# A delta-rule attention and an MLP-mixer on one core: multiplication and addition of an inversion step as separate pieces, and all pieces issued in another order

## The chip, the cores and the metric

The kernel runs on one NeuronCore of one Trainium2 chip. A core has engines that work side by side, each through an instruction queue of its own and in order: TensorE (PE; the loading of its weights is listed as PEld) multiplies matrices into PSUM, VectorE (DVE), ScalarE (ACT) and GpSimd (POOL) work on tiles in SBUF and PSUM, and SyncE (SP) issues the DMAs. The metric is device time in microseconds (us), from start to end of one execution. It is taken in runs of the whole kernel; one execution is also recorded by the hardware profiler, and all rows quoted below come from such a record. TensorE's clock is throttled at times; the granted clock is given as a share of full speed.

## The reference, cut to what matters

Two blocks follow each other, with batch 4, 8 heads, 768 positions, head size 48 (so model width 384), 256 hidden units over tokens and 1536 over channels, all in float32:

```python
k_n = k / (np.linalg.norm(k, axis=-1, keepdims=True) + 1e-06)
for t in range(S):
    kt, vt, bt = (k_n[:, :, t], v[:, :, t], beta[:, :, t, None])
    y[:, :, t] = np.einsum('bhd,bhde->bhe', q[:, :, t], state)
    v_old = np.einsum('bhde,bhd->bhe', state, kt)
    state = state + bt[:, :, :, None] * np.einsum('bhd,bhe->bhde', kt, vt - v_old)
...
xt = x.transpose(0, 2, 1)                  # x: y as (batch, position, 384)
h = np.maximum(xt @ w_tok1, 0.0) @ w_tok2
u = x + h.transpose(0, 2, 1)
h2 = np.maximum(u @ w_ch1, 0.0) @ w_ch2
return (u + h2).astype(np.float32)
```

## The kernel before, in words

**Blocks of the attention.** The positions are cut into chunks of 64, and two chunks make a unit of 128; 4 batches have 24 units, numbered 0 to 23. The effect of one chunk on the state is written with a 64x64 triangular matrix per head, made from the products of the keys with each other, which has to be inverted. So each unit passes these stages, each a generator in the code, and each named by a letter with the unit's number:

- k, `load_kq` (L409 ff., L444): SP loads the keys and queries; the keys also go into a staging tile `kst`.
- p, `prep`: the keys' norms and factors. Its last piece (L592) writes the scaled keys from `kst` into the unit's matrix; for units 0 to 3 it runs on DVE, for the others on POOL.
- c and d, `grams` (L511, L517): TensorE multiplies keys and queries with keys, DVE masks and scales.
- t, `to_parts`: the 32x32 diagonal blocks are put together for the inversion, for units 0 to 5 with copies, for the others with DMAs into a DRAM buffer (`n_dram`).
- i, `invert`: the inversion. It works on rounds of several units: i0 holds units 0 to 3, i1 units 4 and 5, i2 units 6 to 9, i3 10 to 13, i4 14 to 17, i5 18 to 21, i6 22 and 23. All of it is on DVE. Step s multiplies (L739) a column by a row into `sub` and adds (L744) that to the tile `x`. i0 and i1 have 14 such steps, the others 30; the tile has up to 128x240 elements in the middle steps.
- f, `from_parts`, h, `join_16`, j, `join`: the results come back (for later units by DMAs from `w_dram`), and the larger blocks of the inverse are made of them on TensorE, ACT and DVE.
- v, `load_v` (L460, L484): SP loads the values, POOL scales them.

**The recurrence.** r0 to r23 are the chunks of batches 0 and 1, one after the other (`recur`, L920 to L985); r24 to r35 those of batches 2 and 3, two at a time (`recur_pair`, L1009 to L1070). In each, TensorE multiplies the state with keys (`p_k`), DVE subtracts the values, TensorE multiplies by the inverse (`p_w`, first line L944), ACT copies that out of PSUM (L950), TensorE makes the change of the state (`p_s`), DVE subtracts it from the state (L967), and ACT writes the output rows.

**The mixer.** m0 and m1 (`mixer`) are batches 0 and 1; their pieces are put between those of the attention. Batches 2 and 3 are the end of the kernel: T2 and T3 for the part over tokens, A0 to A3, F0 to F3 and B0 to B3 for the part over channels (two units of positions each, with fewer and larger products made of sums; lines L1498 to L1700). w0 to w33 bring in the weights, one 128x384 or 128x256 piece each (`round_weights`): a DMA into one of three buffers `d`, two ACT passes (L286, L287), a DVE shift (L289) and a POOL addition (L293). q and s put aside and sum weights; b is beta; W, S and l belong to the end. x, z and Y are multiplications whose results nobody reads; they keep TensorE busy while nothing else is ready.

**What sets the order.** One string, `order`, lists the pieces by name, `i0*9` for nine pieces of i0, and a loop at the end of the kernel (L1867 ff.) takes one piece of the named generator for each:

```python
for word in order.split():
    name, _, n = word.partition("*")
    for _ in range(int(n or 1)):
        next(jobs[name])
```

A piece is what lies between two `yield`s. Its instructions go to the ends of their engines' queues, so the string is the order in every queue, the DMAs of SP included: an instruction waits for its inputs and buffers, and everything behind it on its engine waits with it. In `invert` one piece is the product and the sum of one step. The weight pieces, keys, queries, values, and the round trips of the inversions all share SP's queue.

Of the kernel before, what the change touches and what calls it, by code (L numbers as in the profile page):

```python
# [23 lines left out]
def kernel(  # L24
# [692 lines left out]
    def invert(rnd):  # L717
# [17 lines left out]
        for s in range(1, m - 1):  # L735
# [8 lines left out]
            nc.vector.tensor_tensor(  # L744
# [1138 lines left out]
```

## Time and profile before

| | |
|---|---|
| median of 3 runs | 624.91 us |
| lowest and highest run | 623.32 and 626.13 us |
| profiled execution: span, first to last instruction | 619.7 us |
| profiled execution: its own time around the span | not listed |
| TensorE busy | 590.3 us (95%), 8733 instructions |
| VectorE busy | 469.1 us (76%), 1160 instructions |
| ScalarE busy | 256.9 us (41%), 682 instructions |
| GpSimd busy | 109.9 us (18%), 150 instructions |
| mean granted TensorE clock | 0.975 |

The span is counted between the first and the last instruction on the core's engines; the time of a run includes what lies around it, so the median is 5.2 us above the span of this execution. An instruction's duration in the profile is that of one execution; a row that ends in x178 is a group of 178 instructions with their sum and mean. A busy engine isn't an engine that is needed: TensorE counts as busy at a low clock too, and with the multiplications that nobody reads.

### The profile page before, as it was taken

How to read it: one execution, taken by the hardware profiler on the slowest of the kernel's cores; microseconds unless marked ns; L12 is line 12 of the kernel's file. 1: busy time of each engine (PE TensorE's matmuls, PEld its weight loads, DVE VectorE, ACT ScalarE, POOL GpSimd, SP SyncE). 2: the span in 40 equal slices, each digit the busy share in tenths (PEclk: the TensorE clock that was granted, in tenths of full speed). 3: DMA queues.
4: the chain of work that ended last, by engine and by line, in shares of the span. 5: the costliest groups of instructions: out<-in, count | busy, mean ns of one | idle time of the engine just before them, and what ended most of it. 6: DMA issues, size and time to landing. Idle time of an engine off the chain costs nothing.

```text
span 619.7 us, 20909 instructions
## 1 busy us (share of the span) xinstructions
PE 590.3 (95%) x8733; PEld 515.9 (83%) x8733; DVE 469.1 (76%) x1160; ACT 256.9 (41%) x682; POOL 109.9 (18%) x150
## 2 busy tenths in 40 slices
PE   8588997999999999999999999999999999999998
PEld 5467875667898988877889888897699999999997
DVE  5987875986889855697566996866888898685874
ACT  8758796448521344223551215415352331414200
POOL 2348264225311122003020120010000000000000
PEclk9878797999999999999999999999999999999999
DMA  9667567667653254454445443135102012020001
GB/s 219 136 135 169 138 142 185 129 155 179 126 114 72 67 116 83 95 113 99 92 87 126 83 95 83 32 66 140 32 2 39 1 21 47 12 52 13 14 26 51
DMA packets 154605, 55.52 MB, mean 90 GB/s; under 512 B 129648, under 2 KB 148976, under 8 KB 154512
## 3 DMA queue, kind: packets, MB, share of 16 engines
q1 hardware_dynamic: 154512, 54.20, 39.1%
q8 instruction: 68, 1.11, 0.8%
q14 instruction: 25, 0.20, 0.1%
HBM read 41.19 MB, written 11.21 MB: 85 GB/s over the span
## 4 chain that ended last, share of the span: by engine, by line
PE 74%; DVE 9%; DMA 4%; ACT 4%; issue 2%; SPq 1%; POOL 1%; DVEq 0%; POOLq 0%; ACTq 0%
PE p_c L1668 13%; PE p_r L1498 13%; PE p_o L1689 10%; PE p_a L1570 7%; PE p_b L1570 6%; PE p_g L511 3%; DMA d<-in_moe_w_ch_dram 3%; PE p_h L1608 3%; DVE sub L739 2%; PE p L1593 2%; DVE x L744 2%; PE p_k L920 2%; PE p L1223 1%; PE p_h L1238 1%; PE p_y L1034 1%
## 5 line engine op out<-in xcount | busy, mean ns | idle before, releaser
L1668 PE MATMUL p_c<-u_t,wc 128*128 128x256 f32 x432 | 101.6, 386 | 0.5 <-issue 0.5
L1668 PEld LDWEIGHTS p_c<-u_t,wc 128*128 128x128 f32 x432 | 79.6, 190 | 11.9 <-issue 1.1
L1689 PE MATMUL p_o<-wc,r 128*128 128x192 f32 x360 | 64.6, 331 | 0.7 <-DVE xb L1628 0.7
L739 DVE TENSOR_TENSOR sub<-x 128x84 f32<-128x84 f32 (+24 forms) x178 | 58.4, 328 | 7.4 <-DMA x<-n_dram 2.8
L744 DVE TENSOR_TENSOR x<-x,sub 128x84 f32<-128x84 f32 (+24 forms) x178 | 58.2, 327 | 6.1
L1689 PEld LDWEIGHTS p_o<-wc,r 128*128 128x128 f32 x360 | 58.4, 190 | 2.3 <-DVE xb L1628 1.3
L1677 ACT ACTIVATE r<-p_c 128x512 f32<-128x512 f32 x36 | 21.4, 596 | 51.2 <-PE p_c L1668 46.1
L511 PE MATMUL p_g<-kq 48*64 48x128 f32 (+1 forms) x704 | 34.9, 283 | 4.0 <-ACT kq L587 3.3
L517 DVE TENSOR_TENSOR gm<-p_g,mb 128x512 f32<-128x512 f32 x44 | 28.9, 683 | 8.1 <-PE p_g L511 7.5
L484 POOL TENSOR_TENSOR v_st<-v_st,nrm 128x384 f32<-128x384 f32 x12 | 10.3, 856 | 131.9 <-DMA v_st<-in_v_dram 104.4
L574 POOL TENSOR_TENSOR mb<-mask_c,cs 128x512 f32<-128x512 f32 x20 | 21.2, 1062 | 67.8 <-DVE cs L552 36.9
L511 PEld LDWEIGHTS p_g<-kq 48*64 48x64 f32 (+1 forms) x704 | 26.5, 137 | 7.6 <-ACT kq L587 4.3
L293 POOL TENSOR_TENSOR wc<-w_f,d 128x384 uint32<-128x384 uint32 x24 | 24.6, 1029 | 42.8 <-ACT d L287 14.1
L1511 DVE TENSOR_TENSOR kq<-kq,p_r 128x384 f32<-128x384 f32 x40 | 21.0, 551 | 10.7 <-PE p_r L1498 8.8
L1498 PE MATMUL p_r<-t_d,wc 128*128 128x192 f32 x160 | 28.8, 326 | 0.0
L1511 DVE TENSOR_TENSOR gm<-gm,p_r 128x384 f32<-128x384 f32 x40 | 21.1, 551 | 8.1 <-PE p_r L1498 5.8
L400 DVE STREAM_TRANSPOSE kq<-pads 128x512 f32<-128x512 f32 x24 | 25.5, 1108 | 2.0 <-PE p_w L1038 1.6
L1498 PEld LDWEIGHTS p_r<-t_d,wc 128*128 128x128 f32 x160 | 26.5, 190 | 0.0
L1689 PE MATMUL p_o<-wc,s 128*128 128x192 f32 x144 | 25.7, 330 | 0.6 <-DVE xb L1628 0.6
L1498 PE MATMUL p_r<-pads,wc 128*128 128x192 f32 x128 | 25.4, 326 | 0.0
L1628 DVE TENSOR_TENSOR xb<-xb,p_o 128x192 f32<-128x192 f32 x42 | 14.6, 348 | 13.0 <-PE p_o L1689 12.6
L1689 PEld LDWEIGHTS p_o<-wc,s 128*128 128x128 f32 x144 | 23.3, 190 | 1.2 <-DVE xb L1628 0.9
(315 smaller groups left out, 1387.1 us busy)
## 6 DMA issues: line engine op xcount, KB each, us to landing
d<-in_moe_w_ch_dram SPq DMA_DIRECT2D x24, 384.0 KB, 4.2
v_st<-in_v_dram SPq DMA_DIRECT2D x96, 48.0 KB, 2.9
out_dram<-xb SPq DMA_DIRECT2D x23, 192.0 KB, 2.1
kst<-in_k_dram SPq DMA_DIRECT2D x64, 48.0 KB, 2.8
n_dram<-gm SPq DMA_DIRECT2D x72, 32.0 KB, 2.3
pads<-in_k_dram SPq DMA_DIRECT2D x24, 96.0 KB, 2.9
pads<-in_q_dram SPq DMA_DIRECT2D x24, 96.0 KB, 2.7
gm<-w_dram SPq DMA_DIRECT2D x72, 32.0 KB, 2.3
```

The lines of the kernel that those rows point to most:

```text
L293: nc.gpsimd.tensor_tensor(out=dst.bitcast(U32), in0=f, in1=lo, op=ALU.add)
L400: nc.vector.transpose(kq_of[p // 2][:, i, :, p % 2].rearrange("f p (s g) -> f p g s", g=G), rows_of[i].rearrange("s p (g d) -> s p g d", g ...
L511: nc.tensor.matmul(p_g[PAR[i ^ cc ^ swap(u)], p], kqt[f, p, cc, 0], kqt[f, p, cc])
L517: nc.vector.tensor_tensor(out=blocks(gm_of(u))[:, :, cc, D:GW].rearrange("s p (two n) -> s p two n", two=2), in0=p_g, in1=made[u][:, :, cc ...
L739: nc.vector.tensor_tensor(out=tmp, in0=y[:, :, 0:s, s : s + 1].to_broadcast([n, k, s, w]), in1=y[:, :, s : s + 1, s + 1 : m].to_broadcast( ...
L744: nc.vector.tensor_tensor(out=y[:, :, 0:s, s + 1 : m], in0=y[:, :, 0:s, s + 1 : m], in1=tmp, op=ALU.add,)
L1498: nc.tensor.matmul(p[:, i], pieces[q // width][:, at : at + 128], f[f"u{n}"], start=first and i == 0, stop=True, skip_group_check=True,)
L1511: nc.vector.tensor_tensor(out=o, in0=o, in1=p, op=op_of(sign))
L1570: nc.tensor.matmul(p, a[:, i], w[:, i // 2, i % 2], start=first and i == 0, stop=True, skip_group_check=True,)
L1668: nc.tensor.matmul(p_c[:, k], piece_of(wc1, cb, f * 128)[:, f * 128 : (f + 1) * 128], u_t[:, cb], start=(cb == 0), stop=(cb == NCB - 1),)
L1677: nc.scalar.activation(r2[:, m], p_c, ACTF.Relu)
L1689: nc.tensor.matmul(p, a[:, m], wc2[:, m, j], start=(start and i == 0), stop=(i == NM - 1), skip_group_check=True,)
```

## The change

In `invert` a `yield` stands between the multiplication and the addition of a step. So a round of inversion has one more piece for each step: i0 and i1 31 in place of 17, the others 62 in place of 32. The order string is another one throughout, with 2788 pieces in place of 2610; apart from those 178 pieces of the inversions each name occurs as often as before. The instructions, their shapes and their tiles stay as they are. Lines after L743 move down by one. The first part of the string, about as far as r11, is shown in both versions, and the end.

```diff
--- before.py
+++ after.py
@@ -741,6 +741,7 @@
                 in1=y[:, :, s : s + 1, s + 1 : m].to_broadcast([n, k, s, w]),
                 op=ALU.mult,
             )
+            yield
             nc.vector.tensor_tensor(
                 out=y[:, :, 0:s, s + 1 : m], in0=y[:, :, 0:s, s + 1 : m], in1=tmp,
                 op=ALU.add,
@@ -1773,76 +1774,95 @@
     jobs["z"] = keep_warm(4)
     jobs["y"] = jobs["Y"] = warm_tiles()
     order = """
-    w10 x*4 z w10*2 z w1*4 k1*3 z k1*3 z b p1 z p1 k0*6 p0*2 b*2 p1 w2 p0*5 p1*2
-    w10 p0*2 z w3 w2 c0*3 p0 w3*2 d0*2 w3 c0 p1 c0 d0*3 k2*3 v1 p1*2 w18 k2*2 p1*2
-    c1*2 d1 k2 p2*2 c1 t0 d1 c1*2 d1*3 t0 p2*8 c2*2 w2 d2 c2*3 Y d2 w2 k3*6 p3
-    d2*2 p3 d2 t1*3 x p3*7 c3 k4*5 k7 w13 w18*2 d3*2 v1*2 v0*2 c3*3 v0 c3 d3*3 t0
-    p4*2 t2*3 x t3*2 p4*2 x t3 i0*2 w13 p4*2 w18 w17*2 i0 k4 i0*9 p4 i0*2 p4*2 c4
-    k8 c4*3 w13*2 w6*2 k5*2 v0 k6 k5*2 i0*2 d4*2 k5 x z d4*3 c4 z*2 p5*2 k5 t4 p5
-    h0 h1 h0 w8*2 h1 Y i0 f0 Y p4 f1 h2*2 p5*3 f0*2 w6 h0*5 k6*5 p6 z f2*2 k8*3 p5
-    w6 p5 p3 p5 j0*3 f1*2 h1*5 j0*2 w8*2 w17 f2 h2*3 v0 t4*2 w17 r0*5 p6 h2*2 c5*2
-    v1 w11*2 j1 p5 k7*2 c5 k7 c5 r0 c5 r0*2 w14*2 v1 w11*2 k7*2 p7 d5*5 r1*5 w14*2
-    p6*2 t5 j1 t5*2 r1*2 j1 j2 p7 h3*2 r1*3 p6*3 i1*2 r2*5 k8*2 f3*2 w9 k9*3 j1*2
-    v2*2 i1*3 j2*2 r2*2 f3 i1*2 p6*3 w16 v2 w16*3 r2*2 h3 r2 i1 d6 r3*5 i1*2 w9*3
-    v2 d6 h3 v2 w0 h3*2 r3 h3 d6*2 w0 d6 j3 c6*5 r3*4 w0 j2 w0 p8*2 j2 r4 p8 r4*4
-    k9*3 j3*2 r4*2 i1*2 w24 i1*2 p7*7 r4 c7 r4 r5*5 k10 p9 k10 p9 c7 r4 c7*3 i1
-    w5*2 p7 r5*2 w24*3 r5*3 j3*2 i1 r6*4 w26 v3*5 p9 k11 r6 d7*5 w26*3 p8*3 t6*2
-    r6*2 w5*2 p8*4 v4*2 t6 i1 r6*3 h5*2 h4*2 k10*2 f4*3 c8*2 k10 p10 w28*2 c8*2 r7
-    c8 r7*3 d8*4 p9 d8 w28 h4*5 p9 t6 r7*2 j4 w28 p9*3 r7*2 p9 w7 d9 w7 v4*2 f5*2
-    w27*2 w7*2 d9*4 c9*2 f5 c9*3 t7*2 t8 r7*2 t7*2 j4*2 v4 p10*2 h5 r8*3 w29 t8*3
-    w29 w27*2 r8*2 w29*2 q3 w29 j4*2 r8 w22*4 t9*3 r8*3 p9 r9 p10 r9*3 t9 v5 h5*3
-    j5 i2 r9 w4*2 r8 h5 i2*5 w4 i2 w19*2 k10 w32 p10*2 w32 v7 k12 m0*2 k11 k12 q0
-    v5*3 p10*2 r9*2 j5*2 k11*3 i2*2 r9 w4 i2 j5 i2*3 p10 v5 r9*2 d10*3 r10 v7*2 j5
-    i2*2 r10*4 w12 i2 k12 i2*2 m0 w32 k11 k12 w32 r10*2 m0 p11 k12*4 w19 p11 r10
-    c10 r10 c10 r10 w33 d10*2 q2 Y r11*4 v7 r11*3 w19 c10 q1 w30 c10 r11 k12*2
-    i2*3 r11 v6*4 i2*5 m0*3 i2*5 q5 i2 m0 p11*4 c10 p11 m0 p11*2 m0*2 k12*2 w12
-    m0*3 v6 f6*3 w12 d11 c11*2 d11*2 c11 w33 c11 d11*2 j6 p12 w12 m0 w33 w30*3
...
-    A3*7 B2*5 A3 B2*2 A3*4 F2*2 F3 B2*7 F3*2 B2*2 F3*2 B2 F3*3 B2*6 F3 F2*2 B3*2
-    F3 B3*10 F3 B2*2 B3*5 F3*4 B3*13
+    x*7 k1 w1 k1 Y k0 k3 k0 k1*4 p1*2 w1*2 b z*2 k3 z*3 k0*4 p0*2 w1 p1 p0 w3 b*2
+    w3 p1 w3*2 p0*3 x p0*4 w2 z p1 d0*5 p1 c0 k2*6 k5 w2 c0*3 w10 c0 p1 k4 p1*2
+    c1 d1*4 p1 k3 p2*2 d1 t0*2 k3 k5 c1*3 p2 k3*2 p2 c1 t0 p2*3 w18 k4 p2 k6 p2
+    c2 d2*3 c2 p2 c2 w10 p3 w10 d2 w2 k4*2 d2 v0 t1 k4 p3*2 w2 k6*2 w10 v1 c2 w6
+    p3 c2 t1*2 p3*5 d3*2 c3 d3 c3*2 w18 c3 w18 d3*2 c3 t2 p4*2 v0 t2*2 t3*2 p4*2
+    k5 k7 k5 t3 i0 k5 w13 i0*4 w18 i0*3 p4 i0*7 w13 w17*2 p4 k4 p3 k7 p4 w13 w6
+    i0*2 p4*2 i0 k8 i0*2 p4 k8*2 i0 d4 v1 k6 k5 d4*2 i0 d4 z i0 z*2 k6 i0*2 c4 i0
+    c4*2 k8 i0 v1 i0 c4 i0*2 w6 w13 d4 c4 t4 h1 v1 h0 h1 w8 h0 p5 i0 p5 f1 f0 w6
+    f0*2 w17*2 Y w11 t4 f1 h2*2 p5*4 h0*2 k6 h0 p5 h0 z j0*2 h0 k7 w8 f2 w8 f1 h1
+    f2*2 j0 h1*3 j1 h1 v0*2 v1 v0 p6 w8 j0*2 p5*3 h2*3 r0*4 h2 r0 p6 c5*2 h2 c5*3
+    k8 r0*2 w14 d5*2 r1*2 p6 k8 w11 d5*2 p6 r1*2 w11*2 r1 d5 j1 k7 k9 k7 k9 p7*2
+    r0 r1 w14 t4 w14 t5*3 h3 r1*2 j2 j1 r1 p6 i1 h3 f3 r2*2 i1 f3*2 p6 j1 j2 j1
+    j2 p6*2 r2 r1 r2 w16 p6 i1 h3 i1 v2 w9 i1*2 p8 w16 h3 d6 r2 i1 r2 v2 i1 v2*2
+    i1*3 d6 r2 h3 i1 r2 d6*2 w16 h3 k10 p6 k10 i1 w14 r2 w0 h3 k9*3 i1*2 k7 c6 w9
+    c6 i1 r3 k10 w16 r3*2 r2 r3 w24 r3 Y w0*2 w9 k10 r3 w9 i1 d6 i1 v3 p7 v3 r3
+    v2 r3*2 j3 c6*3 r3 j2*2 r4 v3 r4*4 i1*6 w0 j3*2 r4*2 i1 w24 p7 i1 p7 r4*2 k10
+    r4 p7*3 p8 r5*4 t6 p9 r5*2 v3 p7 v3 i1 w24 i1 r5 c7*4 k9 r5 i1 c7 r5 r6 p8 r5
+    j3*2 r6 w26 i1 d7 r6 w24 w5 r6*2 v4 d7*3 w26*2 v4*2 d7 w26 p8*4 r6 w5*3 r6
+    p8*3 h5 p9*2 h5 h4 r6 i1 p10 d8*3 h4 t6 d8 f4 t6*2 f4*2 c8*3 r6 v4*2 d8 c8
+    w28 w7 p7 r7*2 w27 r6 r7 w28 r7*2 h4*3 c8 h4*2 t7*3 t8*4 w28*2 p9 r7 p10 r7
+    p9*4 r7 p9 w7 j4 w29 t7 r7 q3 c9*5 d9*5 t9 w7 w27*2 r8*2 f5 t9 r8 j4*2 t9*2
+    f5 j4 r7 f5 j4 p10 r8 w27 r8 w22 w7 p10 r8*2 w4 h5 w29*2 r8*2 r9 h5 r9*3 h5*2
+    j5 w29 j5 w22 j5 r8 w29 r9 w4 w22 i2 h5 w32 i2*3 k10 m0 v6 i2*5 p10 v5 j5 w4
+    i2*4 r9*2 i2*3 Y w22 w19 i2*2 v5 p10 i2*3 r9*2 v5 i2 v5 k12 p10 i2*2 w4 w32
+    k12 j5 k12*2 p10*2 r9 v5 m0 q2 r10 i2 k11*2 w19 r10*4 m0 i2 r10 i2*3 d10*2
+    c10*3 r10 i2*2 r10 c10 r10 k11 m0 k11*3 r11*2 v6 r10 r11 i2 r11 d10 i2*3 r11
+    i2*2 d10 w19 v6 i2*2 Y i2*2 w32 i2*3 k12 i2*3 d10 k12 w30 k12 v7 i2*2 v7 i2
+    r11 v6 r11 i2 q0 r11*2 m0 k12*2 i2*3 w19 i2*2 m0 w32 w33 m0 i2 w12 v7*2 p11
+    i2 q1 i2*2 w30 i2*2 m0 k12 p9 w12 k12 p11 f6 p11 m0 c10 p11*3 m0*2 p11 m0 p11
+    f6*2 p11 w12 w30 f7 w12 m0*2 d11 c11 d11*3 v7 f7*2 w15 c11 w30 f6 d11 j6 f8
...
+    A3*4 B2 A3*3 F2 A3*3 F2*2 A3*2 B2*2 A3*12 F2 A3*12 B2*9 F3*2 B2*4 B1 B2*3
+    F3*3 F2 B2*2 F3 B2*3 F3*2 B2 F3*3 B2 B3*3 F3 B2 B3*4 F3*3 B3*23
     """
     for word in order.split():
         name, _, n = word.partition("*")
```

In the old string the loads and preparations of units 0 to 3 come first, and the first steps of i0 (`i0*2 w13 ...`) in its fifth line; in the new one k1 and w1 come first, keys of units 4 to 7 come earlier, and i0 begins in the seventh line.

101 lines of the change are left out of this document (57 added, 44 removed).

## The prediction

> **What bounds the kernel now.** I read the page first (busy time, slices, chain), then busy time and granted clock by stretches, and then the order of time of single engines where a stretch had holes.
>
> ```profile
> PE 590.3 (95%) x8733; PEld 515.9 (83%) x8733; DVE 469.1 (76%) x1160; ACT 256.9 (41%) x682; POOL 109.9 (18%) x150
> PEclk9878797999999999999999999999999999999999
> PE 74%; DVE 9%; DMA 4%; ACT 4%; issue 2%; SPq 1%; POOL 1%; DVEq 0%; POOLq 0%; ACTq 0%
> L739 DVE TENSOR_TENSOR sub<-x 128x84 f32<-128x84 f32 (+24 forms) x178 | 58.4, 328 | 7.4 <-DMA x<-n_dram 2.8
> L744 DVE TENSOR_TENSOR x<-x,sub 128x84 f32<-128x84 f32 (+24 forms) x178 | 58.2, 327 | 6.1
> ```
>
> TensorE is busy for 95% of the span and carries 74% of the chain. The two lines of the inversion step (L739 multiplies, L744 adds) run 178 times each, a third of a microsecond apiece.
>
> The next rows give, for each stretch, busy time on PE, PEld, DVE, ACT and POOL, then the granted clock, the DMA share and GB/s.
>
> ```profile
> 0.00:20.00 20.00, 16.61 (x197) 11.82 (x197) 11.86 (x40) 16.80 (x45) 4.63 (x17) 1.00 0.81 185
> 20.00:40.00 20.00, 12.31 (x95) 7.76 (x94) 17.80 (x50) 9.93 (x23) 8.97 (x11) 0.74 0.72 164
> 40.00:60.00 20.00, 16.98 (x502) 15.19 (x504) 16.27 (x29) 16.91 (x49) 14.20 (x18) 0.96 0.66 142
> 60.00:80.00 20.00, 18.70 (x539) 16.35 (x535) 16.44 (x48) 16.04 (x46) 7.36 (x10) 0.78 0.58 137
> 80.00:100.00 20.00, 17.73 (x559) 15.38 (x552) 15.14 (x34) 17.58 (x46) 13.08 (x16) 0.99 0.68 154
> 100.00:120.00 20.00, 16.61 (x303) 11.71 (x304) 15.55 (x47) 9.81 (x27) 4.77 (x7) 0.76 0.67 163
> 120.00:440.00 320.00, 314.76 (x5504) 264.81 (x5497) 238.22 (x610) 120.16 (x347) 56.91 (x74) 1.00 0.46 101
> 440.00:620.00 180.00, 176.56 (x1068) 172.85 (x1067) 137.85 (x308) 49.64 (x105) 0.00 (x0) 1.00 0.11 24
> ```
>
> This splits the kernel in two. From 120 us on, TensorE is short of full by 320 - 314.76 = 5.2 us up to 440 and by 3.4 us after it, with the clock at 1.00. No order of the same matmuls can win more there than these 8.7 us. Before 120 it is idle for 120 - 98.9 = 21 us, and the clock is down to 0.74, 0.78 and 0.76 in three of the six stretches. So the end is set by **how early the full stretch begins**, and this hangs on the recurrence steps r0 to r11, with DVE, ACT, POOL and the one DMA queue of SP around them.
>
> **The change, part by part.**
>
> *The yield.* It adds no instruction: the orders hold the same pieces, except that i0 and i1 grow from 17 to 31 and i2 to i6 from 32 to 62, 178 more, one for each L739. Its own cost is 0: DVE, which executes them, gets the same 1160 instructions. What it can give is that an urgent DVE piece stands behind one half of a step and not a pair, 0.4 us for the longest steps (rows below).
>
> *The order up to r0.* The first 120 us have nearly the same pieces in both orders, moved by a few places, but the SP queue differs. I counted its DMAs: the transfer that w13 waits for goes from 22nd to 33rd, that of w17 from 28th to 34th, the queries of block 4 from 29th to 35th, the last values of block 0 (needed by r0) from 34th to 52nd. In front now stand the keys of blocks 5 and 6 and w6. On DVE, p3's last piece (L592) and w13's shift now stand inside the first inversion, after its 14th half step; p3's stood behind the inversion.
>
> ```profile
> 12.36 0.55 DVE L592 TENSOR_TENSOR wc<-kst,cs 128x384 f32<-128x384 f32 x1
> 46.13 1.15 POOL L293 TENSOR_TENSOR w<-w_f,d 128x384 uint32<-128x384 uint32 x1 [0.35 <-issue]
> 46.42 1.29 DVE L592 TENSOR_TENSOR gm<-lent,cs 128x384 f32<-128x384 f32 x1
> 29.80 0.60 SPq L444 DMA_DIRECT2D kst<-in_k_dram  x1
> d<-in_moe_w_ch_dram SPq DMA_DIRECT2D x24, 384.0 KB, 4.2
> 32.58 0.28 DVE L739 TENSOR_TENSOR sub<-x 128x112 f32<-128x112 f32 x1
> 47.76 1.91 SPq L444 DMA_DIRECT2D lent<-in_k_dram  x3
> v_st<-in_v_dram SPq DMA_DIRECT2D x96, 48.0 KB, 2.9
> 51.11 0.83 POOL L460 TENSOR_TENSOR v_st<-v_st,nrm 128x384 f32<-128x384 f32 x1
> 52.00 0.68 PE L944 MATMUL p_w<-v_st,wc 64*64 64x48 f32 x15
> 52.00:99.00 47.00, 42.74 (x1272) 37.71 (x1270) 36.92 (x92) 40.18 (x109) 26.85 (x34) 0.89 0.68 157
> ```
>
> The first inversion: L592 costs 0.55 us (alone) to 1.29 us (beside POOL). The Trainium skill, "SBUF — State Buffer", section "Who interferes with whom", says that a VectorE instruction with two SBUF inputs and a GpSimd instruction that reads SBUF exclude each other; the 1.29 beside POOL's L293 agrees, and by it this item would be 0.7 us dearer wherever POOL is running. The 33rd DMA was issued at 29.80; with 4.2 us to landing, w13's data is there at 34.0, ACT's first pass adds half a microsecond, and DVE stands at this place at 32.6 + 0.55. So DVE waits up to 1.4 us and the first inversion ends 0.55 to 2.0 us later than before. Queued behind it are t16 and with it h0, j0 and r0.
>
> The values of block 0: the 52nd DMA was issued at 48.4 (second of the row at 47.76). With 2.9 us to landing and 1.0 us for POOL's two instructions (the longer one is the 0.83 at 51.11), r0 starts at 52.3 where it started at 52.00; POOL now also takes block 1's values first, about one more: 53.3. Both paths meet in r0, so the larger counts, not the sum: +0.3 to +2.0, I take +1.2. Between 52 and 99 the busiest engine after TensorE, ACT, has 47 - 40.18 = 6.8 us without work; a late r0 can be made up there. I keep **+0.5** at r8, between 0 (all hidden) and +2.0 (cover gone). Bounds of the start itself (k1's keys are now the first DMA, two weight transfers later): ACT is busy 16.80 of the first 20 us, and the same ACT pieces stand before the first inversion in both orders, so 0.
>
> *The order from r8 to r11*, where I see the gain. The window rows have the columns of before; the others are start, duration, engine.
>
> ```profile
> 99.00:102.00 3.00, 0.99 (x30) 0.63 (x26) 0.72 (x2) 1.07 (x3) 0.59 (x1) 0.59 0.30 55
> 102.00:105.00 3.00, 2.12 (x48) 1.88 (x48) 0.99 (x4) 1.01 (x5) 2.47 (x3) 0.50 0.70 193
> 105.00:108.00 3.00, 3.00 (x10) 2.08 (x9) 2.56 (x11) 1.05 (x4) 0.37 (x1) 0.50 1.00 299
> 108.00:111.00 3.00, 3.00 (x14) 1.61 (x12) 2.79 (x9) 2.08 (x5) 0.97 (x2) 0.71 1.00 232
> 101.02 0.55 ACT L286 ACTIVATE d<-d 128x384 f32<-128x384 f32 x1 [1.93 <-DMA d<-in_moe_w_ch_dram]
> 102.05 0.32 ACT L950 COPY rw_t<-p_w 128x192 f32<-128x192 f32 x1
> 106.94 0.44 ACT L286 ACTIVATE d<-d 128x256 f32<-128x256 f32 x1 [3.88 <-DMA d<-in_moe_w_tok_dram]
> 111.67 0.56 ACT L286 ACTIVATE d<-d 128x384 f32<-128x384 f32 x1 [1.42 <-DMA d<-in_moe_w_ch_dram]
> 112.56 0.30 ACT L950 COPY rw_t<-p_w 128x192 f32<-128x192 f32 x1
> 105.41 0.18 DVE L739 TENSOR_TENSOR sub<-x 128x30 f32<-128x30 f32 x1
> 112.15 0.38 DVE L744 TENSOR_TENSOR x<-x,sub 128x210 f32<-128x210 f32 x1
> 114.15 0.35 DVE L967 TENSOR_TENSOR ss_t<-ss_t,p_s 128x192 f32<-128x192 f32 x1
> 117.28 0.41 DVE L744 TENSOR_TENSOR x<-x,sub 128x240 f32<-128x240 f32 x1
> 120.37 0.34 DVE L967 TENSOR_TENSOR ss_t<-ss_t,p_s 128x192 f32<-128x192 f32 x1
> ```
>
> ACT's queue holds r8's copy (L950 at 102.05) behind w22's passes, and these wait for a DMA; r9's copy (112.56) stands behind w32's, which wait again. TensorE, which waits for these copies, is idle 3.00 - 0.99 + 3.00 - 2.12 = 2.9 us, and at the low clock loses 0.99 x 0.41 + 2.12 x 0.5 + 3 x 0.5 + 3 x 0.29 = 3.8 us more: 6.7 us in all. In the new order r8's copy stands ahead of w29 and w22, and r9's ahead of w32 and w19. If the whole hole closes, that is -6.7, the upper bound.
>
> What is late next: r9's state update (L967, 114.15) is on DVE, now behind 20 half steps of i2 (it was behind 24). The 20th, at 112.15, ends at 112.5, and i2 begins at 105.41 in both unless its input lands sooner. So r9's update moves by 114.15 - 112.55 = 1.6 us. r10's stands behind 30 half steps, where 34, two weight shifts and a reduction stood; the 30th (117.28 + 0.41 = 117.69) ends 2.7 us ahead of 120.37. I take **-2.5**: between the leads at r9 and r10, near the latter, which is nearest to the start of the full stretch. The other bound is 0, if i2's input is late by the same amount.
>
> ```profile
> 60.00:63.00 3.00, 3.00 (x54) 2.49 (x49) 2.45 (x3) 2.18 (x6) 1.78 (x3) 0.50 0.77 179
> ```
>
> The clock part of the hole. In 99 to 105 the low clock (0.59, 0.50) follows idle time on TensorE; in 60 to 63 it is 0.50 with TensorE busy 3.00 of 3. The Trainium skill, "TensorE: Matmul & The Clock Gate", section "Part 1: The HAM clock gate (the "warmup" mystery)", says that the clock halves after an idle window of some 3.4 us. The first pair of numbers agrees, the second shows that a busy stretch can have it too. By that rule a shorter idle time at 99 would give the whole 3.8 us of clock back at once; by the row it need not. The -2.5 holds none of it beyond the update's lead; rival 1 holds all.
>
> *From 120 us on.* Both orders hand the same matmuls to TensorE. The 5.2 us of idle time up to 440 are small pieces, and DVE has 320 - 238.2 = 81.8 us free there, so most of what the finer pieces allow finds nothing to win. I take **-0.3**, since the wait for a step's second half, 0.4 us, can fall away where an urgent DVE piece stood behind a pair; bounds -5.2 (all idle time goes) and +1.0 (three pieces that now come behind one half step more, 0.35 each). After 440 no inversion is left and DVE has 42 us free: 0, with bounds -3.4 (its idle time) and +2.0 (six more of the 0.35 us pieces ahead of TensorE's next input). The DMAs that were moved here run at a DMA share of 0.46 and less, where the early stretches work at 0.58 to 0.81: 0, inside the same bounds.
>
> **The sum.** 0 (yield) + 0.5 (late r0) - 2.5 (r9, r10) - 0.3 = -2.3. On the profiled execution's span, 619.7, that is 617.4. The median of the runs, 624.91, lies 5.2 us above that span, time around it that the change doesn't touch. So **622.6 us**.
>
> **The rivals.**
>
> *1: the whole hole closes.* r8's and r9's copies no longer wait on ACT behind weight data, TensorE runs on through 99 to 111, and its clock stays up: 624.9 - 6.7 = 618.2. For it: the three ACT waits of 1.93, 3.88 and 1.42 us stand right ahead of these copies, and two of the passes are now behind them. Against it: w22's first pass and w4's are still ahead of r9's copy, and DVE is busy 2.56 and 2.79 of 3 us from 105 on, so the inversion's steps set the pace next. It needs i2 to begin some 3 us before 105.41, so that its 20th half step is done by 109.5.
>
> *2: slower, by the SP queue.* SP issues in order. Keys of block 7 go into the buffer that p3's last piece reads, which now stands inside the first inversion; while they wait, the DMAs behind them wait too, among them w17's and block 0's values. One landing of a weight (4.2 us) on top of the 2.0 above makes r0 6.2 us late. Of this TensorE could make up at most 47 - 42.7 = 4.3 us up to 99, if every idle moment were usable; in a chain of steps I count half, 2.1, so 4.1 is kept at r8. The lead of 2.5 is gone then too, because r9's update waits for its matmul and not for DVE: 624.9 + 4.1 = 629.0. For it: SP issues weights, keys, queries and values in one queue, and in 20 to 40 TensorE already has only 12.3 of 20 us busy. Against it: the DMA engines are at 0.58 to 0.81, so what is issued lands soon. It decides from r0 at 57.6 on: half of that 5.6 us is 2.8, what the rest of the sum gives.
>
> *3: nothing is left of it.* The copies come earlier, but i2's half steps are as late as before, since their input comes through a DMA round trip (n_dram, 2.3 us each way) that ends at 105.4 again, and the updates of r9 and r10 still stand behind 20 and 30 of them with other pieces between: 624.9. For it: DVE's stretch 105 to 111 is nearly full in the old order. Against it: fewer pieces stand ahead in the new one.
>
> **How the numbers follow.** What a measurement of this kernel can tell from no change is about 0.5%, 3.1 us: 621.8 to 628.0. The forecast has 0.38, and its own range is 620.5 to 625.0 (from twice the lead at r9 to a lead that is just spent): 0.10 of that is below 621.8, 0.28 within. Rival 1 has 0.24, all faster. Rival 2 has 0.20, all slower. Rival 3 has 0.18: 0.03 faster, 0.12 within, 0.03 slower, because so many pieces were moved that the bounds of the late stretches (-3.4, +2.0) can fall either way. Together 0.37 faster, 0.40 the same, 0.23 slower. The range goes from 616.0 (rival 1 with some 2.2 of the 5.2 us after 120) to 629.5 (rival 2 with half a microsecond from the late stretches).
>
> **What would show it.** In the changed kernel's profile, step by step: 178 instructions each on L739 and L744 with the same mean durations (no cost of the yield); the first inversion's end and w13's shift inside it, with a DVE wait of at most 1.4 us for ACT or a DMA; r0's first L944 at 52.3 to 54.0 (rival 2: 57.6 or later, with idle time on SP's queue for DVE before it); r8's and r9's L950 with less ACT idle time ahead of them than 7.2 us in sum; the updates L967 of r9 and r10 some 1.6 and 2.7 us ahead of 114.15 and 120.37 less r0's half microsecond; TensorE's busy time in 100 to 120 at 18 to 19 in place of 16.61 with the clock at about 0.8 (rival 1: above 0.9; rival 3: as before); and in 120 to 440 a TensorE idle time of about 5. The forecast is wrong if the full stretch begins earlier by over 5 us or not at all, if TensorE's idle time after 120 changes by over 2 us, or if one of the low clock stretches (20 to 40, 60 to 80) comes or goes without any wait that explains it.

## The result, and the profile after

The changed kernel takes 644.1 us (median of 4 runs, 641.8 to 645.8), the one before 624.1 us in the same comparison: ratio 1.031, 95% interval 1.027 to 1.0345. The forecast was 622.6 us with a range of 616.0 to 629.5. The profiled execution has a span of 644.0 us, 24.3 more. In the four runs of the changed kernel the time lies 1.7 to 2.2 us above the span, not 5.2 as taken for the kernel before: so the execution of before that was profiled ran some 2 to 3 us quicker than its median run, the changed one some 2 us longer, and the rows of the two profiles show some 4 us more than the 20.0 that the change costs. Medians and ratios below leave out single executions in a slower state (three of over 900 us among them), so a median can differ by a few tenths from the one that an expectation names.

The page of the changed kernel, the lines that answer to those of before (lines after L743 have moved down by one):

```profile
PE 592.4 (92%) x8733; PEld 514.4 (80%) x8733; DVE 464.9 (72%) x1160; ACT 254.9 (40%) x682; POOL 109.8 (17%) x150
PEclk9969999899999999999899999998999999999999
L739 DVE TENSOR_TENSOR sub<-x 128x84 f32<-128x84 f32 (+24 forms) x178 | 58.4, 328 | 23.9 <-DMA x<-n_dram 19.0
L745 DVE TENSOR_TENSOR x<-x,sub 128x84 f32<-128x84 f32 (+24 forms) x178 | 61.6, 346 | 5.3
```

TensorE does the same 8733 matmuls in 2.1 us more, so the other 22 us are idle time. The number that stands out is the last of the L739 line: DVE waited 23.9 us ahead of the inversions' multiplications, 19.0 of it for the DMA that brings an inversion its input; it was 7.4 and 2.8.

The same stretches as before: busy time on PE, PEld, DVE, ACT and POOL, then granted clock, DMA share and GB/s.

```profile
0.00:20.00 20.00, 17.76 (x172) 12.90 (x172) 9.93 (x33) 14.28 (x38) 4.30 (x17) 1.00 0.73 166
20.00:40.00 20.00, 6.85 (x96) 5.62 (x96) 18.29 (x48) 11.30 (x27) 9.76 (x11) 0.75 0.67 152
40.00:60.00 20.00, 18.45 (x372) 13.34 (x368) 12.45 (x28) 13.50 (x39) 9.29 (x13) 0.91 0.61 134
60.00:80.00 20.00, 17.02 (x602) 14.48 (x599) 16.16 (x49) 16.83 (x48) 9.51 (x12) 1.00 0.61 133
80.00:100.00 20.00, 17.44 (x521) 15.08 (x514) 16.21 (x38) 16.67 (x45) 11.92 (x15) 1.00 0.60 139
100.00:120.00 20.00, 13.54 (x351) 9.92 (x348) 13.75 (x42) 12.54 (x35) 6.81 (x8) 0.97 0.78 200
120.00:440.00 320.00, 302.74 (x5094) 255.17 (x5093) 228.34 (x593) 111.39 (x321) 57.37 (x74) 0.99 0.43 94
440.00:644.00 204.00, 198.59 (x1556) 187.84 (x1554) 149.75 (x335) 58.37 (x133) 0.83 (x1) 0.99 0.14 35
```

TensorE's idle time is 28.9 us up to 120 (21 before), 17.3 between 120 and 440 (5.2), and 5.4 after that (3.4): 8 + 12 + 2. The low clock of 0.78 and 0.76 in 60 to 80 and 100 to 120 is absent in this trace; but with the same order there, e5's trace has 0.74 in 100 to 120 (experiments below), so its absence is not shown to be the order's work. The larger loss of idle time came after 120, where the forecast had seen nothing to win or lose.

### The profile page after: what moved, and what is told of

Read it like the earlier page. It is cut to its first block, busy times and chain, and to the rows that moved or that the text cites. A ratio compares the mean times of both kernels' runs of the same rounds, so it can differ in the third digit from the quotient of the medians.

```text
span 644.0 us, 20888 instructions
## 1 busy us (share of the span) xinstructions
PE 592.4 (92%) x8733; PEld 514.4 (80%) x8733; DVE 464.9 (72%) x1160; ACT 254.9 (40%) x682; POOL 109.8 (17%) x150
## 4 chain that ended last, share of the span: by engine, by line
PE 34%; DVE 8%; DMA 3%; SPq 3%; issue 1%; ACT 1%; POOL 0%; DVEq 0%; ACTq 0%; POOLq 0%
PE p_r L1499 12%; PE p_a L1571 6%; PE p_b L1571 6%; DVE x L745 3%; DVE sub L739 3%; PE p_o L1690 2%; PE p L1224 1%; PE p_h L1239 1%; DMA x<-n_dram 1%; PE p_h L1373 1%; PE p L1306 1%; SPq L391 1%; DVE kq L400 1%; DMA kst<-in_k_dram 1%; DVE s L1649 1%
## 5 line engine op out<-in xcount | busy, mean ns | idle before, releaser
L739 DVE TENSOR_TENSOR sub<-x 128x84 f32<-128x84 f32 (+24 forms) x178 | 58.4, 328 | 23.9 <-DMA x<-n_dram 19.0
L745 DVE TENSOR_TENSOR x<-x,sub 128x84 f32<-128x84 f32 (+24 forms) x178 | 61.6, 346 | 5.3
L574 POOL TENSOR_TENSOR mb<-mask_c,cs 128x512 f32<-128x512 f32 x20 | 21.2, 1062 | 135.5 <-DVE cs L552 107.5
L511 PE MATMUL p_g<-kq 48*64 48x128 f32 (+1 forms) x704 | 33.5, 278 | 6.4 <-ACT kq L587 4.5
L1678 ACT ACTIVATE r<-p_c 128x512 f32<-128x512 f32 x36 | 21.3, 595 | 43.7 <-PE p_c L1669 40.4
L517 DVE TENSOR_TENSOR gm<-p_g,mb 128x512 f32<-128x512 f32 x44 | 29.0, 682 | 9.0 <-PE p_g L511 8.7
L539 ACT ACTIVATE ksq<-kst 128x384 f32<-128x384 f32 x18 | 9.5, 526 | 54.4 <-DMA kst<-in_k_dram 54.3
L1512 DVE TENSOR_TENSOR gm<-gm,p_r 128x384 f32<-128x384 f32 x40 | 21.3, 551 | 8.6 <-PE p_r L1499 6.4
```

Source lines behind the costliest of these rows:

```text
L511: nc.tensor.matmul(p_g[PAR[i ^ cc ^ swap(u)], p], kqt[f, p, cc, 0], kqt[f, p, cc])
L517: nc.vector.tensor_tensor(out=blocks(gm_of(u))[:, :, cc, D:GW].rearrange("s p (two n) -> s p two n", two=2), in0=p_g, in1=made[u][:, :, cc ...
L739: nc.vector.tensor_tensor(out=tmp, in0=y[:, :, 0:s, s : s + 1].to_broadcast([n, k, s, w]), in1=y[:, :, s : s + 1, s + 1 : m].to_broadcast( ...
L745: nc.vector.tensor_tensor(out=y[:, :, 0:s, s + 1 : m], in0=y[:, :, 0:s, s + 1 : m], in1=tmp, op=ALU.add,)
L1512: nc.vector.tensor_tensor(out=o, in0=o, in1=p, op=op_of(sign))
L1678: nc.scalar.activation(r2[:, m], p_c, ACTF.Relu)
```

## The experiments

**The time by stretches.** Seven kernels are put together from both orders: one order up to the last piece of a step, then the other with what is left. (At a seam, pieces that the first order had already issued drop out, and those that it still owes come first.) e3, the seam in the order string:

```diff
 w19 c10 q1 w30 c10 r11 k12*2 i2*6 r11
-v6*4 i2*10 m0*3 i2*2
+v6*3 Y i2*9 v6 i2 m0 i2*5
...
```

> The old order up to the last piece of r11, then the new order with what is left. The trace of the changed kernel has r11's end 4.4 us late and the end 24.3 us late. If the 20 us after r11 come from the late order itself, this gives about 624 + 20 = 644, 638 to 646. If they are an after-effect of the late start (buffers and transfers that are late once stay late), it gives 624 to 630.

e4, the same the other way round:

```diff
 k12 w30 k12 v7 i2*2 v7 i2 r11 v6 r11 i2 q0 r11*2
-m0 k12*2 i2*3 w19 i2*2 m0 w32 w33
+p9 v7 w12 w32 p11 k12 p11 w33 v7 w19
...
```

> The new order up to the last piece of r11, then the old order with what is left. If the loss is local to each part, r11's 4.4 us late end stays and nothing is added: about 628.5, 626 to 631. If the new early order costs more later (after-effect), 635 to 645. If the full stretch after r11 makes the early delay up, 623 to 626.

e3 took 639.2 us, ratio 1.025 (1.020 to 1.031); e4 629.3 us, 1.009 (1.006 to 1.012). 2.5% and 0.9% make 3.5%, the whole change 3.1%, the same within the intervals: the late part costs some 16 us by itself, and the early one some 6.

e15 and e18 move the seam of e3 to the last piece of i4 and of i6:

```diff
 i4*5 r24*3 r25*2 m1 v14 i4*3
-v14*2 p18*2 r25 m1*2 p19 m1*5
+p18 m1*3 p18 m1 p19 v14*2 p19 r25
...
```

> The old order up to the last piece of i4, then the new order. With the new order from r11 on, 639.2 was measured, and its trace had i4's load 6.7 us late and the end 16.5. If the late loss is local to its stages, 632 to 635 remains (the 15 less the 6 to 7 up to i4). If most of it comes from before i4's end, 624 to 629; if from after it, 636 to 640.

```diff
 v21 r32 i6*13
-m1*2 r30 r32*6 v21*2 s v21 s
+s r30 v21*2 v22 v21 r32*4 m1 f22
...
```

> The old order up to the last piece of i6, then the new order: the end of the kernel (steps r33 to r35, T2, T3, A, F, B) in the new order. The prediction costed that part at 0, bounds -3.4 and +2.0. 622 to 626 agrees; with the new order from i4's end on it was 632.3, so 629 or more would put that loss into the end and not into i5 and i6.

e15: 632.3 us, 1.011 (1.007 to 1.0155). e18: 625.95 us, 1.0045 (1.002 to 1.007). So of the late 16 us some 9 go back to the order between r11 and the end of i4, 4 to that up to the end of i6, and 3 to that of the end of the kernel; by the intervals, give or take 4, 3 and 2 us. This divides the order and not the time: what is put off in one part can be paid for in a later one. In e3's trace no single place holds the loss. TensorE idles 15.6 us between 160 and 480 us, 3.7 before, and in six of the eight stretches of 40 us it is between 1.1 and 3.6.

e13 takes the new order up to r7's last piece, e16 only from i0's first piece to r7's last, e10 only from there to r10's last; the rest is the old order.

```diff
 w7 w27*2 r8*2 f5 t9 r8 j4*2 t9*2 f5 j4 r7
-f5 j4 p10 r8 w27 r8 w22 w7 p10
+k11 w7 f5 p10 h5 w29 w27 r8*2 w29*3
...
```

> The new order up to r7's last piece, then the old order with what is left. If the late start (i0 2 to 3 us later, r0 4 to 5) is made up before r11, as the prediction's cover has it, 623 to 626. If it is kept, 627 to 630.

```diff
 t2 x t3*2 p4*2 x t3 i0
-i0*2 w13 p4*2 w18 w17*2 i0*2 k4 i0*12
+x k5*2 k6*3 w6 k5*3 i0*4 w18 i0*3 p4 i0*4
...
```

> The old order up to i0's first piece, the new one from there to r7's last piece, then the old order. The new order up to r7 followed by the old one was 628.75 us, 4.6 above the old order. If the late start (i0 3 us later) is what was kept, 623 to 626 is left. If the order from i0 to r7 (p3's last piece and w13 inside i0, the values of block 0 late on SP) does it, 627 to 630.

```diff
 f5 c9*3 t7*2 t8 r7*2
-t7*2 j4*2 v4 p10*2 h5 r8*3 w29 t8*3 w29 w27*2 r8*2 w29
+v4 t7 t8*3 p10 w29 t7 q3 t9 w27 r8*2 t9 r8 j4*2 t9*2 j4*2
...
```

> The old order, except that after r7's last piece the new order is followed up to r10's last piece, and then the old order with what is left. The prediction saw its gain there: r8's and r9's copies ahead of the weights' passes on ACT. If that lead is real and kept, 620 to 623 us, and ACT's waits for weight data ahead of these copies are gone. If it is swallowed by DVE's half steps of i2, 623 to 626; if the new arrangement there costs time, 626 to 630.

e13: 628.5 us, 1.006 (1.0025 to 1.009). e16: 629.7 us, 1.011 (1.0085 to 1.014). e10: 629.4 us, 1.008 (1.005 to 1.011). Without the late start (e16) the loss is no smaller, so the order between i0 and r7 is enough for it; but e16's seam puts eight issues for k5, k6 and w6, which the new order has before i0, right behind i0's first piece, which makes the transfers behind them later still. And r8 to r10, where the forecast had its gain, cost 5 us when changed alone. e13's and e10's losses make 9 us and e4 has 6; the difference lies within the intervals, so whether the early stretches share their loss is open.

**The start.** In the changed kernel's trace i0 begins at 29.7 us, not 26.7; DVE and ACT waited for beta. (In nine traces with the old order up to r7 it begins at 26.7 to 28.2, median 27.7; in five with the new one at 28.9 to 29.9, median 29.7: 2.0 us are the order's.) e7 puts beta's DMA first, e9 takes 2.4 us of multiplications that nobody reads out of TensorE's queue ahead of beta's product.

```diff
-    x*7 k1 w1 k1 Y k0 k3 k0 k1*4 p1*2 w1*2 b z*2 k3
+    b x*7 k1 w1 k1 Y k0 k3 k0 k1*4 p1*2 w1*2 z*2 k3
```

> The new order with beta's DMA issue first of all (it stood behind six others and was issued at 5.05 us; DVE and ACT waited for beta until 12.3 and 11.8 us). Theory: the start was late by 3.0 us through beta, so i0 begins at 27 to 28 in place of 29.7 and the time falls by 2 to 3 us, to 641 to 642. Rival: the late start is made up or hidden before r11 and the time stays at 643 to 645.

```diff
-    x*7 k1 w1 k1 Y k0 k3 k0 k1*4 p1*2 w1*2 b z*2 k3
+    x*4 k1 w1 k1 k0 k3 k0 k1*4 p1*2 w1*2 b z*2 k3
...
-    k5 k7 k5 t3 i0 k5 w13
+    k5 k7 k5 t3 i0 x*3 Y k5 w13
```

> The new order with three of its seven first filler multiplications (x) and the first Y moved behind the first piece of i0, so that ahead of beta's product on TensorE stand four x and five z, as in the old order. Theory: the start was late because TensorE, in order, had 10.2 us of fillers ahead of beta's product (7.8 before), not because of beta's DMA; then beta's product begins at 7.8, i0 at 26.7 to 27.5 in place of 29.7 (or 28.8, as some runs have it), and the time falls by 1.5 to 3 us, to 641 to 643. Rival: other work limits the start, i0 stays at 28.8 or later and the time at 643 to 645.

e7: 643.9 us, 1.032 (1.027 to 1.037); e9: 643.3 us, 1.029 (1.025 to 1.032). Neither moved i0 (30.0 and 30.1). What sets the new start is open, and so is what it costs by itself.

**What makes i0 to r7 late.** TensorE's waits between 24 and 50 us (the total, how many, the longest) of before, of the changed kernel and of e16:

```profile
PE p_t L582 <- DMA pads<-in_q_dram: 5.4, 1, 5.4
```

```profile
PE p_t L582 <- DMA pads<-in_q_dram: 9.0, 1, 9.0
```

```profile
PE p_t L582 <- DMA pads<-in_q_dram: 11.4, 1, 11.4
PE p_g L511 <- ACT kq L587: 1.0, 1, 1.0
```

And DVE's between 28 and 50 us in e16:

```profile
DVE gm L517 <- PE p_g L511: 4.0, 1, 4.0
```

The queries of block 4 come 35th on SP and not 29th. TensorE stands for them with p4's transposition, the products of block 4 (c4, d4) follow late, and DVE waits 4.0 us for these with c4's mask (1.3 in the changed kernel), behind which the last piece of i0 stands. In e16 i0 takes 21.3 us from its first to its last instruction, in the changed kernel 18.7, before 16.9. That i0 and the wait grow together agrees with this chain; no run puts the queries back alone, so their share of the 4 to 7 us is not measured.

**r8 to r10.** e14 is e10 with i2's load moved ahead of two weight transfers:

```diff
-    t9 j4*2 p10 r8 w27 r8 w22 p10 r8*2 w4
+    t9 i2 j4*2 p10 r8 w27 r8 w22 p10 r8*2 w4
```

> As the run with only r8 to r10 in the new order (629.7), but i2's load stands on SP right behind the last block of t9, ahead of the transfers of w22 and w4. Theory (i2 begins 4 us later behind these two transfers, and i2's end sets r12): i2's first half step at 106 or earlier, i2's end at 135 or earlier, and the time 624 to 627. Rival (i2's load waits for t9's blocks or DVE's order sets its end): 628 to 631.

The issue of that load, and its time from issue to landing (least, median, most of one), in before (where no landing is listed in this view), in e10 and in e14:

```profile
L733 SPq DMA_DIRECT2D x<-n_dram x1: 338/338/338, 101.8 to 101.8; - x1
```

```profile
L733 SPq DMA_DIRECT2D x<-n_dram x1: 326/326/326, 102.4 to 102.4; - x1
DMA to landing us min/median/max: 6.2/6.2/6.2
```

```profile
L733 SPq DMA_DIRECT2D x<-n_dram x1: 337/337/337, 101.3 to 101.3; - x1
DMA to landing us min/median/max: 3.6/3.6/3.6
```

Behind the 640 KB of w22 and w4 the load takes 2.6 us longer to land. Moved ahead of them, i2 begins at 106.8 and ends at 136.3 (e10: 108.7 and 139.1), earlier, though not by all that the theory had; the time, 630.6 us, 1.010 (1.006 to 1.014), shows no gain. So the load does land later behind these two, and it isn't shown to be what this stretch costs.

**SP's order as a whole.** e1 and e2 mix the orders another way: the pieces that are nothing but one DMA issue in about the sequence of the one order, all computing pieces in that of the other.

> The changed kernel, with the pieces that are nothing but one DMA issue (keys, queries, values, weights, the inversions' round trips, beta) put back into about their old sequence; every other piece stays in the new order, the split steps too. Theory 1 (the order of SP's queue made the loss: beta's transfer at the start, and the blocks and loads of the inversions i3 to i5 behind values and keys of later units) expects 622 to 630 us and the waits of L739 for its DMA at 3 us or less in place of 16.5. Theory 2 (the new order on DVE, ACT and TensorE made the loss) expects 640 to 648. In between: both have a share.

> The other way round: the old order of all computing pieces (the two halves of a step next to each other), with the pieces that are nothing but one DMA issue in about their new sequence. Theory 1 (SP's queue) expects 638 to 648 us, most of the 20 us lost; theory 2 (the order on DVE, ACT and TensorE) expects 622 to 628.

e1: 656.3 us, 1.052 (1.043 to 1.061). e2: 662.0 us, 1.063 (1.056 to 1.0695). Both are slower than both kernels, and neither theory's times came. So a mix adds a loss of its own, and the two don't tell in which queue the loss of the change arises.

**The way to i4's input.** SP's issues (start, duration) and then DVE, in the changed kernel between 254 and 269 us:

```profile
256.06 2.76 SPq L474 DMA_DIRECT2D v_st<-in_v_dram  x3
258.91 1.02 SPq L391 DMA_DIRECT2D pads<-in_k_dram  x2
260.03 2.92 SPq L686 DMA_DIRECT2D n_dram<-gm  x5
262.99 0.60 SPq L474 DMA_DIRECT2D v_st<-in_v_dram  x1
264.24 0.34 SPq L733 DMA_DIRECT2D x<-n_dram  x1
```

```profile
256.92 1.29 DVE L517 TENSOR_TENSOR gm<-p_g,mb 128x512 f32<-128x512 f32 x2 [2.21 <-PE p_g L511]
259.18 0.55 DVE L1649 TENSOR_TENSOR r<-r 128x384 f32<-128x384 f32 x1
268.58 0.19 DVE L739 TENSOR_TENSOR sub<-x 128x30 f32<-128x30 f32 x1 [8.84 <-DMA x<-n_dram]
268.68 0.55 DVE L1649 TENSOR_TENSOR s<-r 128x384 f32<-128x384 f32 x1
```

The same place before:

```profile
245.39 1.29 DVE L517 TENSOR_TENSOR gm<-p_g,mb 128x512 f32<-128x512 f32 x2 [0.16 <-PE p_g L511]
253.06 0.56 DVE L1648 TENSOR_TENSOR s<-r 128x384 f32<-128x384 f32 x1 [6.38 <-ACT r L1677]
254.86 0.18 DVE L739 TENSOR_TENSOR sub<-x 128x30 f32<-128x30 f32 x1
```

From c17's mask (L517) to i4's first half step it takes 268.58 - 256.92 = 11.7 us, 9.5 before, and now the mixer's piece (L1649 at 268.68) stands behind the waiting half step. But of the 13.7 us that i4 begins later, 11.5 are there at c17's mask already; only 2.2 arise on this way. e5 moves ten issues behind i4's load; e6 besides these five behind i5's, and i6's load ahead of what stood between it and t23. In both, v12's scaling comes behind r24's first use of it, so r24 works with unscaled values; the instructions are the same. e11 has the same three moves, with v12 scaled in time, on top of e3.

```diff
-    v12*2 p17 r23 p17 t15 v12 p17 v12 j13 r23 v13 p17 m0 r23 c17 k18 v12 k18 c17*5 t17*4
+    p17 r23 p17 t15 p17 j13 r23 p17 m0 r23 c17*6 t17*4
...
-    m0 r23 m0*2 v13 m0*2 i4 j13 i4
+    m0 r23 m0*4 i4 v13*2 v12*4 v13 k18*2 v13 j13 i4
```

> The new order with one thing moved: the ten DMA issues for values of pairs v12 and v13 and the first two keys of k18, which stand in SP's queue between r22 and the load of i4, go right behind that load (and v12's scaling on POOL behind v13's). Ten issues of 0.6 us stand ahead no longer. Theory SP-round-trip (values and keys of later units ahead of the way from c17 through DRAM to i4 cost what was lost there) expects L739's wait for its DMA at i4 to fall from 8.8 us to 4 or less and the time from 644.1 to 637 to 640. The rival, that i4's late input is covered by other work or that the late keys of block 17 set it, expects 642 to 646.

> As the run before, and the same at the two later inversions: the four values of v17 and the first key of k22 behind the load of i5, and the load of i6 right behind the last block of t23 and ahead of six other issues. Theory SP-round-trip expects 3 to 6 us less than the run before it, 632 to 636; the rival, that the losses at i5 and i6 have another cause (the loads of keys for blocks 19 to 22 late, DVE's order), expects a change of under 1.5 us from it.

> The old order up to r11, then the new order, with the three round trips put first on SP: the values v12, v13 and two keys of k18 behind i4's load, v17 and one key of k22 behind i5's, i6's load right behind t23. The same without these moves was 639.2 us, 15 above the old order. Theory SP-round-trip: 8 to 12 of the 15 come back, 627 to 631, and L739's waits for its DMA fall from 16.0 us to under 8. Rival (the order on DVE and the keys of blocks 19 to 22 cost most): 634 to 640.

e5: 638.6 us, 1.024 (1.018 to 1.030), within what its theory forecast, with the wait at i4 at 6.0 us (4 or less forecast); beside the changed kernel's 1.031 a gain of 4 us, give or take 4. e6: 639.9 us, 1.027 (1.021 to 1.033), nothing more. e11: 638.9 us, 1.022 (1.019 to 1.026), beside e3's 1.025. DVE's waits for that DMA between 125 and 480 us fell, e3 first, then e11:

```profile
DVE sub L739 <- DMA x<-n_dram: 16.0, 4, 7.9
```

```profile
DVE sub L739 <- DMA x<-n_dram: 10.7, 3, 5.8
```

5.3 us of waits less, and some 2 us of time, give or take 4. So the theory that these moves bring back most of the late loss (8 to 12 us) falls. Counted from r23's copy on ACT, i4's first half step starts after 10.7 us in e11's trace (12.8 in e3's), but its last one ends after 41.2 (40.8): what i4 gains at its start is lost within it.

e12 and e17 go the other way: they put ten, and four, of these issues into the *old* order, ahead of t17 and i4's load.

```diff
-    c17 r23*2 c17 t17*2 m0*8 p17 t17*2 i4*5 v12 m0 k18 v15*2
+    c17 r23*2 c17 v12 k18*2 v12*3 v13*4 t17*2 m0*8 p17 t17*2 i4*5 m0 v15*2
```

> The old order with ten DMA issues (the values v12 and v13, two keys of k18) moved from behind i4's load to ahead of the blocks t17, where the new order has them. Theory (issues ahead of the way through DRAM to i4 cost their 0.6 us each, since TensorE has no other work ready): 627 to 631. Rival (TensorE has work enough; SP's order there is hidden): 623 to 626.

> The old order with only the four values v12 ahead of the blocks t17 and i4's load. In the run with ten issues SP stood 10.8 us behind the load of v15, whose buffer r24 had to free, and k18's keys stood behind it. If the loss there was that stall, this gives 624 to 628 (four issues of 0.6 us, partly hidden). If it grows with each issue ahead of the load, 627 to 631.

e12: 636.3 us, 1.019 (1.015 to 1.023), 12 us for ten issues of 0.6 us. e17: 625.1 us, 1.005 (1.0025 to 1.0075). The waits of SP (240 to 285 us), ACT (240 to 290) and PE (240 to 285) in e12:

```profile
SPq L474 <- PE p_w L1039: 10.8, 1, 10.8
...
ACT ksq L539 <- DMA kst<-in_k_dram: 19.2, 2, 14.7
...
PE p_s L1053 <- ACT rw_t L1044: 4.7, 1, 4.7
PE p_o L1690 <- DVE xb L1629: 3.6, 1, 3.6
```

The first wait of PE can be read from bottom to top: TensorE waits 4.7 us for r24's copy on ACT; that stands in ACT's queue behind the squares of k18 (L539), which wait for keys; the keys stand on SP behind a load of values that waits for a buffer which r24 frees. The other one, 3.6 us, is for an addition (L1629) that stands on DVE behind i4's first half steps, and these waited 4.9 us for their input. The stretch from r23 to i4's end, in e12 and then in before:

```profile
246.00:297.00 51.00, 42.59 (x421) 35.37 (x421) 30.79 (x89) 8.55 (x23) 3.40 (x6) 0.90 0.32 71
243.00:282.00 39.00, 38.74 (x425) 31.53 (x424) 30.11 (x86) 8.95 (x23) 3.46 (x6) 1.00 0.43 91
```

It holds the whole 12 us: TensorE idles 8.1 us more, about the two waits, and needs 3.9 more for about the same matmuls at a clock of 0.90. With four issues SP waits 5.0 us at the same place, ACT 3.3 in two waits and TensorE not at all for that copy, and 3 us remain, as was forecast for the case that the stall is the cost. The price of a moved DMA is thus not its issue time. No run makes the stall alone, with the ten issues in place, so the chain is read from one trace and not varied link by link.

**The halves.** e8 puts each addition back behind its multiplication, in the new order.

```diff
-    c4*2 k8 i0 v1 i0 c4 i0*2 w6
+    c4*2 k8 v1 i0*2 c4 i0 w6
...
```

> The new order with each inversion step's addition moved back right behind its multiplication. If the split has no price and no gain of its own, 642.5 to 646. If finer DVE pieces won something in it, 647 to 652. If pieces put between the halves did the harm (DVE waits between the halves), 636 to 641.

e8: 650.4 us, 1.040 (1.034 to 1.046), against 1.031 (1.027 to 1.0345) with the halves apart. The split gains in the new order, by 5.7 us going by the ratios, give or take 4; it isn't what made the kernel slower.

## Why the prediction was wrong, point by point

*The yield costs nothing:* held. 178 L739 with a mean of 328 ns as before; L745 has 346 in place of 327 ns, 3.4 us in all, but in e3, with the same split, 335.

*Finer pieces win 0.3 us:* too small for this order; e8 shows 5.7, give or take 4. The wait of half a step was priced for a few pieces, not for a whole order made around it.

*i0 longer by 0.55 to 2.0:* held, 18.7 against 16.9 us. *r0 at 52.3 to 54.0:* 57.1 in the changed kernel's trace, as its first line shows:

```profile
L945 PE MATMUL p_w<-v_st,wc x16: 218/218/253, 57.1 to 57.9; 64*64 64x48 f32 x16
```

Of the 5.1 us, 3.0 are the later start of i0, costed at 0 because the same ACT pieces stood ahead of it; ACT did less work there (14.28 of the first 20 us in place of 16.80), since it waited. But the 52.00 that I counted from was an early one, by chance: nine traces with the old order have r0 at 52.0 to 55.5, median 54.5, five with the new one at 55.7 to 57.3, median 56.9. So the order's share is some 2.4 us, little above the 2.0 of the forecast's bound.

*+0.5 kept at r8:* this step failed. e13 and e16 keep 3.6 and 7 us of time. The cover, ACT's 6.8 idle microseconds between 52 and 99, doesn't help a chain that waits for another engine. I had counted the queries of block 4 among the later transfers and priced the two beside them only.

*-2.5 at r8 to r11:* this step failed; e10, where this part alone is new, loses 5 us. Its first half held, as these rows of ACT and DVE show:

```profile
103.62 0.32 ACT L951 COPY rw_t<-p_w 128x192 f32<-128x192 f32 x1 [0.18 <-PE p_w L945]
106.44 0.56 ACT L286 ACTIVATE d<-d 128x384 f32<-128x384 f32 x1 [0.94 <-DMA d<-in_moe_w_ch_dram]
111.30 0.32 ACT L951 COPY rw_t<-p_w 128x192 f32<-128x192 f32 x1 [1.48 <-PE p_w L945]
```

```profile
109.87 0.19 DVE L739 TENSOR_TENSOR sub<-x 128x30 f32<-128x30 f32 x1 [2.49 <-DMA x<-n_dram]
117.47 0.35 DVE L968 TENSOR_TENSOR ss_t<-ss_t,p_s 128x192 f32<-128x192 f32 x1
123.57 0.35 DVE L968 TENSOR_TENSOR ss_t<-ss_t,p_s 128x192 f32<-128x192 f32 x1 [1.39 <-PE p_y L960]
```

```profile
99.00:102.00 3.00, 2.03 (x86) 1.61 (x82) 2.19 (x5) 2.61 (x7) 0.84 (x1) 1.00 0.87 197
111.00:114.00 3.00, 2.96 (x60) 2.01 (x52) 2.76 (x10) 2.68 (x7) 0.95 (x2) 1.00 0.72 194
114.00:117.00 3.00, 0.23 (x1) 0.00 (x0) 2.79 (x7) 1.86 (x5) 0.83 (x1) 1.00 0.73 169
117.00:120.00 3.00, 2.04 (x19) 1.41 (x20) 2.83 (x9) 0.00 (x0) 0.00 (x0) 0.78 0.67 114
120.00:123.00 3.00, 3.00 (x65) 1.89 (x65) 2.04 (x5) 0.32 (x1) 0.00 (x0) 0.65 0.81 118
```

ACT no longer waits for weights ahead of r8's copy, and 0.94 us ahead of r9's; the hole at 99 is smaller, at full clock. The updates of r9 and r10, forecast 1.6 and 2.7 us earlier, came 3.3 and 3.2 later (117.47 and 123.57). 4.4 us of that had come before: r7's copy on ACT starts at 96.5 and not 92.1. Counted from it, i2 begins when I had kept it (after 13.3 us in both), and the two updates come 1.1 and 1.2 us earlier. So a part of the lead was there. It did not last: the hole opened again at 114 to 117, where DVE is busy 2.79 of 3 us with half steps and TensorE 0.23, because r10's products wait for r9's update behind the half steps. TensorE's wait for these updates between 100 and 160 us, before and after:

```profile
PE p_k L920 <- DVE ss_t L967: 0.5, 1, 0.5
```

```profile
PE p_k L921 <- DVE ss_t L968: 4.2, 2, 3.7
```

From r7's to r11's copy it is 30.6 us in both traces, with 7.0 us of idle time on TensorE in place of 5.3. That is rival 3: the lead is swallowed by i2's steps. Then more was lost, where the sum had stopped: it took r10's update for the start of the full stretch, but r12 needs i2's results. From r11's copy to i2's last half step it is 11.2 us in place of 8.6, with 2.2 us of idle time on TensorE in place of none (1.8 of it for a DVE addition, L1613, among the half steps), and from r11's to r12's copy 24.4 to 24.7 us in five traces of the new order against 21.1 to 21.2 in seven of the old. In e4, where only what stands up to r11 is new, it is 23.4; in e10 23.8. So some 2 us are lost there by the order up to r11. What else e10's 5 us are is not settled: e14 takes i2's late load away and shows no gain. (The way back from `n_dram`, which rival 3 has at 2.3 us, took 4.0 in the kernel before; its argument doesn't hang on it.)

*-0.3 from 120 us on, bounds -5.2 and +1.0:* the largest error. e3 measures 16 us for what comes after r11. The premise was that the end is set by how early the full stretch begins; it stayed full only in the old order, and the bound of +1.0 priced three half steps and no wait for a load. I counted free time (81.8 us on DVE) and took it for cover. In queues that run in order, free time behind a waiting instruction covers nothing, as the row at 268.58 shows, and the lead of some loads over their use had shrunk: ACT's idle time ahead of the keys' squares (L539), before and after:

```profile
DMA kst<-in_k_dram: 4.7, 4
```

```profile
DMA kst<-in_k_dram: 54.3, 8
```

ACT has time, but DVE waited behind it for 14.9 us in that view, 4.7 before. *0 after 440, bounds -3.4 and +2.0:* e18 has +2.8 (1.2 to 4.5).

Rival 2, the slower side, had the right kind of mechanism (an SP queue in which what is needed next stands behind what isn't) and a price of 6.2 us at r0, 4.1 of it kept: 629.0 in all, 15 us short. What it describes is seen in part there, and at i4 and in e12 later; a rival that is one place can't price an order that is new throughout. Which of these places make up the late 16 us stays open: moving the round trips of i4 to i6 forward shortened the waits and not the time.

## What to carry to other kernels

When a whole order is replaced, price the late stretches too, even if they look full: for each DMA that is moved, compare its lead over the first instruction that needs it and what stands behind that instruction. Free time of an engine is no cover for a chain through in-order queues; ten DMA issues in the wrong place cost twice their 6 us of issue time, in two waits of TensorE and a lower clock beside them. Hybrids of two orders, cut at a step, tell roughly which part of the order a loss goes back to; mixing one queue's order with the other's did not. And a time read from one trace is no base for a forecast of 2 us: compare it from a nearby point of the same trace, or in several traces.
